# Splitting the first input load over two queues and moving a bias transpose in a fused attention and MLP kernel

One core of a Trainium2 chip. The metric is the device time of one execution in microseconds (us), median of several runs.

## The reference, cut to what matters

```python
x  = A_x                                # [1, 2048, 640] bf16
xn = layernorm(x)                       # per row of 640
return x + attention(xn, wqkv, wo) + mlp(xn, w1, b1, w2, b2)

def mlp(x, w1, b1, w2, b2):             # w1 [640, 1536], w2 [1536, 640]
    h = gelu_tanh(x @ w1 + b1)
    return h @ w2 + b2
```

The linear attention (32 heads) comes after the first MLP half in the kernel and is not touched by the change.

## The kernel before: the parts that matter

Tokens come in 16 tiles of 128 rows. The kernel starts with the MLP's first half on tiles 0 and 1, since that needs only x, W1 and the bias b1. The loads are issued from two queues, SyncE's and ScalarE's:

```python
KA = 2
dma_x(0, 1)                                                     # SyncE: x0, 128 rows
dma_w("scalar", b1tmp[:], B_b1..., r_b1tmp)                     # ScalarE: bias, 12 rows of 128
dma_w("scalar", W1[:, 0:KA, 0:FW], w1v[:, 0:KA, 0:FW], r_W1A)   # ScalarE: first W1 rows, 256 KB
dma_x(1, 1)                                                     # SyncE: x1
dma_w("sync", W1[:, KA:DT, 0:FW], w1v[:, KA:DT, 0:FW], r_W1[0]) # SyncE: rest of W1 block 0
dma_w1(1); dma_x(2, 1); dma_w1(2); dma_x(3, 1); ...             # SyncE: W1 block 1, x2, W1 block 2, x3
```

TensorE meanwhile multiplies zeros (`filler`), which does nothing but keep it active, and transposes the bias. VectorE takes the LayerNorm statistics of x0 and of x1, and then normalizes x0:

```python
filler(6)            # six zero matmuls of 512 columns
b1_step()            # bias transpose on TensorE, copy on ScalarE
filler(3)
ln_stats(0)          # VectorE, GpSimd: statistics of x0
ln_half(1, 0)        # VectorE: statistics of x1
ln_half(1, 1)
norm_part(0, 0, CA, r_xnA)      # VectorE: normalize x0, in two parts
norm_part(0, CA, D, r_xnB)
ln_aggr(1)
dA, sA, bA = transp_part(0, 0, 2, r_xnA)     # TensorE: transposes of x0
filler(1)
dB, sB, bB = transp_part(0, 2, DT, r_xnB)
# ... [cut] copies, normalize x1, transposes of x1, products of tile 0, of tile 1
units(0, 2, JQ, 2 * JQ + 1)     # from here on 256 tokens at once
```

## Time and profile before

| | before |
|---|---|
| time, median of 3 (range) | 206.53 us (206.44 to 206.76) |
| span of the profiled execution | 205.2 us |
| x0 landed / x1 landed | 3.15 / 3.83 us |
| x0 transposes / first products | 5.54 / 6.40 us |
| TensorE at full clock from | 4.96 us |

All times within an execution are counted from the start of its span. TensorE has work without a gap from 6.4 us to the end, so the end moves with anything that delays it there. "Landed" is the last of the semaphore increments of a load in the trace, one for each DMA engine that took part. The clock is the trace's record of the granted TensorE clock. The profile lines stand in the prediction.

### The profile page before, as it was taken

To read this page: it belongs to the slowest core of one execution; us is meant where nothing else is said; L and a number is where in the kernel's file an instruction comes from. 1 tells how busy PE (TensorE), PEld (TensorE's weight loads), DVE (VectorE), ACT (ScalarE), POOL (GpSimd) and SP (SyncE) were. 2 spreads that over 40 slices of the span, in tenths; PEclk is the share of its full clock that TensorE was granted. 3 is DMA by queue.
4 is the path that set the end of the run, shared out by engine and by line. 5 is a ranking of instruction groups with operands and counts; after the bars stand their busy time and mean duration, and the time that the engine had idled before them with its cause. 6 is when DMAs were issued, how large, how long until landed. Compare 5 with 4: busy or idle time off the path is not lost.

```text
span 205.2 us, 3767 instructions
## 1 busy us (share of the span) xinstructions
PE 201.8 (98%) x1517; PEld 138.6 (68%) x1517; DVE 113.2 (55%) x231; ACT 72.5 (35%) x136; POOL 15.0 (7%) x46
## 2 busy tenths in 40 slices
PE   7999999999999999999999999999999999999996
PEld 2789987444457777777756565677777777777775
DVE  4678677200006888999388888464773422523332
ACT  3588887666676554211143675000000000000000
POOL 3143334300000000000000000000000000000000
PEclk9999999999999999999999999999999999999999
DMA  5993954499940000000300034781112111010012
GB/s 181 350 352 79 70 96 91 78 355 268 285 164 0 0 0 3 0 0 3 64 0 2 3 71 89 244 279 43 67 64 71 54 43 50 32 35 32 32 35 66
DMA packets 26664, 19.23 MB, mean 94 GB/s; under 512 B 13766, under 2 KB 26646, under 8 KB 26646
## 3 DMA queue, kind: packets, MB, share of 16 engines
q1 hardware_dynamic: 26350, 18.72, 33.5%
q10 hardware_dynamic: 296, 0.27, 0.4%
q8 instruction: 12, 0.20, 0.4%
q14 instruction: 6, 0.05, 0.1%
HBM read 12.72 MB, written 2.62 MB: 75 GB/s over the span
## 4 chain that ended last, share of the span: by engine, by line
PE 96%; DVE 1%; DMA 1%; issue 0%; DVEq 0%
PE ps L644 34%; PE ps L358 24%; PE ps L495 11%; PE ps L531 11%; PE ps L543 11%; PE ps L680 2%; PE ps L390 1%; DMA xPK<-in_A_x_dram 1%; DVE stats L314 1%; PE ps L557 1%; PE ps L575 1%; PE ps L591 1%; PE ps L379 0%; PE ps L342 0%; DVE xn_tm L372 0%
## 5 line engine op out<-in xcount | busy, mean ns | idle before, releaser
L644 PE MATMUL ps<-W,HG 128*128 128x320 bf16 x360 | 51.0, 300 | 0.0
L358 PE MATMUL ps<-xnT,W 128*128 128x256 bf16 (+2 forms) x385 | 50.6, 294 | 0.0
L644 PEld LDWEIGHTS ps<-W,HG 128*128 128x128 bf16 x360 | 35.1, 98 | 14.2 <-issue 0.4
L358 PEld LDWEIGHTS ps<-xnT,W 128*128 128x128 bf16 x385 | 33.8, 98 | 16.0 <-DMA W<-in_B_w_dram 0.2
L362 ACT ACTIVATE HG<-ps,b1c 128x256 bf16<-128x256 f32 (+2 forms) x77 | 38.0, 515 | 12.8 <-PE ps L358 10.4
L663 DVE TENSOR_TENSOR out_sb<-ps,xnT 128x640 bf16<-128x640 f32 x15 | 12.4, 825 | 35.0 <-PE ps L644 33.6
L482 ACT ACTIVATE ek<-ps 128x512 bf16<-128x512 f32 (+1 forms) x36 | 23.2, 644 | 19.6 <-PE ps L543 10.4
L483 DVE TENSOR_SCALAR ek<-ek 128x512 bf16<-128x512 bf16 (+1 forms) x36 | 11.0, 307 | 26.3 <-ACT ek L482 24.8
L543 PE MATMUL ps<-xnT,Wqkv 128*128 128x512 bf16 x100 | 22.8, 380 | 0.0
L644 PE MATMUL ps<-Msb,PQ 128*128 128x320 bf16 x150 | 22.3, 300 | 0.0
L495 PE MATMUL ps<-Wqkv,xnT 128*128 128x320 bf16 x160 | 21.9, 300 | 0.0
L531 PE MATMUL ps<-xPK,xn_tm 128*128 128x320 bf16 x160 | 21.9, 300 | 0.0
L495 PEld LDWEIGHTS ps<-Wqkv,xnT 128*128 128x128 bf16 x160 | 15.7, 98 | 6.2
L531 PEld LDWEIGHTS ps<-xPK,xn_tm 128*128 128x128 bf16 x160 | 15.7, 98 | 6.1
L644 PEld LDWEIGHTS ps<-Msb,PQ 128*128 128x128 bf16 x150 | 14.7, 98 | 5.7
L543 PEld LDWEIGHTS ps<-xnT,Wqkv 128*128 128x128 bf16 x100 | 11.3, 118 | 8.5
L314 DVE BATCH_NORM_STATS2 stats<-xPK 128x6 f32<-128x320 bf16 x32 | 14.7, 469 | 3.1 <-DMA xPK<-in_A_x_dram 3.1
L485 DVE SCALAR_TENSOR_TENSOR PQ<-ps,ek 128x512 bf16<-128x512 f32 x20 | 13.8, 692 | 2.1
L485 DVE SCALAR_TENSOR_TENSOR xPK<-ps,ek 128x640 bf16<-128x640 f32 x16 | 13.2, 825 | 1.7
L518 DVE TENSOR_TENSOR Msb<-Msb,xPK 128x640 f32<-128x640 f32 x14 | 11.6, 825 | 0.5
L324 POOL TENSOR_TENSOR rstd<-aggr,mhalf 128x1 f32<-128x1 f32 x16 | 9.1, 567 | 15.8 <-DVE aggr L322 15.8
L535 ACT ACTIVATE W<-ps 128x640 bf16<-128x640 f32 x5 | 3.5, 703 | 18.2 <-PE ps L531 18.2
(61 smaller groups left out, 90.5 us busy)
## 6 DMA issues: line engine op xcount, KB each, us to landing
xnT<-in_A_x_dram SPq DMA_DIRECT2D x4, 640.0 KB, 6.8
Wqkv<-in_A_wqkv_dram SPq DMA_DIRECT2D x3, 800.0 KB, 6.6
out_dram<-out_sb SPq DMA_DIRECT2D x15, 160.0 KB, 1.8
W<-in_B_w_dram SPq DMA_DIRECT2D x1, 1920.0 KB, 15.8
W<-in_B_w_dram SPq DMA_DIRECT2D x2, 640.0 KB, 7.4
xPK<-in_A_x_dram SPq DMA_DIRECT2D x2, 640.0 KB, 9.0
Wo<-in_A_wo_dram SPq DMA_DIRECT2D x1, 750.0 KB, 12.4
xPK<-in_A_x_dram SPq DMA_DIRECT2D x4, 160.0 KB, 4.6
```

What stands on the lines that cost most here:

```text
L314: Pl.ins(v, lambda e: e.bn_stats(stats[:, s, 6 * h:6 * h + 6], x_in[:, t, h * HW:(h + 1) * HW]), reads=[r_x[t]], writes=[r_stats[s][h]])
L358: Pl.ins("tensor", [(lambda e, k=k: e.matmul(bank(b, 0, w), W1[:, k, jb * P:(jb + 1) * P], xnT[:, k, tok], start=(k == 0), stop=(k == DT - ...
L362: Pl.ins("scalar", lambda e: e.activation(HG[:, jb, tok], bank(b, 0, w), ACT.Gelu_apprx_tanh, bias=b1c[:, jb:jb + 1]), reads=[B_[b], r_b1c ...
L482: Pl.ins("scalar", lambda e: e.activation(e2, src, ACT.Exp), reads=br, writes=[r_ek[s]])
L483: Pl.ins(v, lambda e: e.tensor_scalar(et, et, 1.0, 1e-6, ALU.min, ALU.add), reads=[r_ek[s]], writes=[r_ek[s]])
L485: Pl.ins(v, lambda e: e.scalar_tensor_tensor(out=d2, in0=src, scalar=0.0, in1=e2, op0=ALU.max, op1=ALU.add), reads=br + [r_ek[s]], writes= ...
L495: fns.append(lambda e, k=k, h=h, b=b, t=t: e.matmul(bank(b + h, 0, HW), xnT[:, k, t * P:(t + 1) * P], Wqkv[:, k, D + h * HW:D + (h + 1) * ...
L518: Pl.ins(v, lambda e, t=t: e.tensor_tensor(out=zsum, in0=zsum, in1=PK[:, t, :], op=ALU.add), reads=[r_PK[t], r_zsum], writes=[r_zsum])
L531: Pl.ins("tensor", [(lambda e, t=t, h=h, b=b, f=f: e.matmul(bank(b + h, 0, HW), xn_tm[:, t, f * P:(f + 1) * P], PK[:, t, h * HW:(h + 1) * ...
L543: Pl.ins("tensor", [(lambda e, k=k, j=j, b=b: e.matmul(bank(b), Wqkv[:, k, j:D:DT], xnT[:, k, cc], start=(k == 0), stop=(k == DT - 1))) fo ...
L644: return lambda e: e.matmul(bank(b + h, 0, HW), l, r[:, h * HW:(h + 1) * HW], start=(i == 0), stop=(i == JT + DT - 1))
L663: Pl.ins(v, lambda e: e.tensor_tensor(out=halves(out_sb[:, s, :]), in0=pair(b), in1=halves(x_res[:, t, :]), op=ALU.add), reads=B_[b:b + 2] ...
```

## The change

The intent: x0 is the first load and everything waits for it, so let two queues bring one half each; bring the first W1 rows directly behind; let the small bias come later, as it is needed last. Its transpose moves behind the zero matmuls, of which eight stand ahead of LayerNorm instead of nine.

```diff
-        dma_x(0, 1)
+        HP = P // 2
+        r_x0b = R_("x0b")
+        dma_w("sync", x_in[0:HP, 0, :], xv[0:HP, :], r_x[0])
+        dma_w("scalar", x_in[HP:P, 0, :], xv[HP:P, :], r_x0b)
+        dma_w("scalar", W1[:, 0:KA, 0:FW], w1v[:, 0:KA, 0:FW], r_W1A)
         dma_w("scalar", b1tmp[:], B_b1.rearrange("(a p) -> a p", p=P), r_b1tmp)
-        dma_w("scalar", W1[:, 0:KA, 0:FW], w1v[:, 0:KA, 0:FW], r_W1A)
         dma_x(1, 1)
 # ... [cut: the statistics of x0 wait for r_x0b as well]
-        filler(6)
+        filler(8)
         b1_step()
-        filler(3)
         ln_stats(0)
```

More of the change, by code (lines that the diff above doesn't have):

```diff
@@ L314, in ln_half @@
             Pl.ins(v, lambda e: e.bn_stats(stats[:, s, 6 * h:6 * h + 6], x_in[:, t, h * HW:(h + 1) * HW]),
-                   reads=[r_x[t]], writes=[r_stats[s][h]])
+                   reads=[r_x[t]] + ([r_x0b] if t == 0 else []), writes=[r_stats[s][h]])
             if h == 0:
```

## The prediction

> **What bounds the kernel now.** I read the page's busy shares first, then the chain of work that ended last, then the start of the trace engine by engine, because the change touches nothing after the first 6 us. Shares and the 40 slices:
>
> ```profile
> span 205.2 us, 3767 instructions
> PE 201.8 (98%) x1517; PEld 138.6 (68%) x1517; DVE 113.2 (55%) x231; ACT 72.5 (35%) x136; POOL 15.0 (7%) x46
> ...
> PE   7999999999999999999999999999999999999996
> ```
>
> TensorE holds the end. It is short of full only in the first slice (5.1 us) and the last, so a change to the loads can win only part of the first 6 us, about 3% of the span. The first pieces of the chain, in order of time, give that part its order (columns: start, length, what, all us):
>
> ```profile
> 0.80 2.35 DMA xPK<-in_A_x_dram
> ...
> 3.17 0.90 DVE stats L314 x2
> ...
> 5.14 0.36 DVE xn_tm L372
> ...
> 5.54 0.29 PE ps L379 x2
> ...
> 6.40 0.94 PE ps L390 x14
> ```
>
> The first x tile is issued at 0.80 and lands at 3.15. LayerNorm of it follows on VectorE and GpSimd (3.17 to 5.50), then the transposes from 5.54, then the first real matmuls at 6.40. So x0's landing looks like the bound, and 3.25 us of fixed work lie between it and the first product (6.40 - 3.15). The same stretch on TensorE, in the timeline:
>
> ```profile
> 1.25 2.74 PE L301 MATMUL ps<-warm 128*128 128x512 bf16 x6 [1.25 <-DVE warm L270]
> 3.92 0.19 PE L306 MATMUL ps<-ident,b1tmp 12*128 12x12 bf16 x1
> 4.04 1.25 PE L301 MATMUL ps<-warm 128*128 128x512 bf16 x3
> 5.54 0.29 PE L379 MATMUL ps<-ident,xn_tm 128*128 128x128 bf16 x2 [0.25 <-DVE xn_tm L372]
> ```
>
> Nine zero matmuls and the bias transpose end at 5.29; TensorE is idle for 0.25 us before the x0 transposes, so none of those is on the path. Most important for me is what comes later: two waits for loads that the change does not shorten, one in the weight loads of TensorE, one on VectorE.
>
> ```profile
> 11.34 0.44 PEld L358 LDWEIGHTS ps<-xnT,W 128*128 128x128 bf16 x5 [0.17 <-DMA W<-in_B_w_dram]
> ```
>
> ```profile
> 9.46 0.89 DVE L314 BATCH_NORM_STATS2 stats<-xPK 128x6 f32<-128x320 bf16 x2 [1.09 <-DMA xPK<-in_A_x_dram]
> 11.41 0.45 DVE L335 TENSOR_SCALAR xn_tm<-xPK,aggr,rstd 128x640 bf16<-128x640 bf16 x1 [0.76 <-POOL rstd L324]
> ```
>
> The third block of W1 (issued at 3.29, landed 8.0 us later, at 11.29) is needed by hidden block 8 at just that time: the weight load waits 0.17 us for it, which costs the matmuls some 0.05 us (their starts are 0.159 us apart there, 0.109 before). x2 lands at 9.43, and its LayerNorm ends at 11.86 (11.41 + 0.45), as TensorE comes to its transposes (11.91). TensorE therefore meets the load stream at 11.3 to 11.9 with no slack. After that it has no gap.
>
> **What the Trainium skill says.** "DMA: Bandwidth & Descriptors", section "Issuing engines are not separate DMA queues": loads from ScalarE's and SyncE's queues run on the same 16 DMA engines, and a second issuer saves only issue time. The trace fits: the order in which data moved (x0, x1, first W1 rows, rest of the block) is the order of issue over both queues (0.80, 1.25, 1.45, 1.72). The same page, "Queues, rings and completion order" and "Why a DMA increments its semaphore by 16 and not by 1": each engine works through one queue's descriptors in order, 128 or 64 rows are spread over 16 engines, 12 rows over the lowest 12. Fitting it, the bias tile has 12 landings after its issue in the trace (2.13 to 2.64), x0 has 16 (2.69 to 3.15). "TensorE: Matmul & The Clock Gate", Part 1: the array starts at half clock and is released after some 3.4 us of activity, in a window that does not start with the kernel. Here zero matmuls of 512 columns start 0.43 us apart at first, and the clock record goes to full at 4.96, 3.7 us after the first one.
>
> **The change, part by part.**
> 1. *x0 in two halves on two queues.* Of x0's 2.35 us, about 1.0 lie before its first bytes (they move at about 1.8), 1.0 are spent moving 160 KB, and the rest is landing. At the 300 GB/s of the filled queues, 160 KB would take 0.5 us, so the ramp is worth at most 0.5 us. Both halves still use all 16 engines, each with 4 rows per queue in place of 8 in one, and 16 more queue entries have to be made. The bias load no longer goes first. I expect 0.15 us (estimate; 0 to 0.35), so landing at 3.0.
> 2. *The chain behind it* moves along unchanged: transposes at 5.39 instead of 5.54, first products at 6.25 instead of 6.40. Its limit is the first W1 rows: 15 of their 16 landings came by 4.91, the last, from one slow engine, at 6.04 (1.45 + 4.6). So at most 0.3 us can be won there. They remain second on ScalarE's queue and are issued at about the same time.
> 3. *Zero matmuls.* 9 become 8 ahead of LayerNorm: 1.25 + 8 x 0.43 = 4.69 for their end. The removed 0.43 us lay in idle time: no gain. The clock may be released later because TensorE is idle from about 4.9 to 5.4; I give that little weight.
> 4. *The bias*, now third on ScalarE's queue, issued near 1.86, some 1.06 us later than before, and one more issue of 0.4 to 0.6 us before the 1.28 us table load. ScalarE is idle from 4.33 to 5.87, so that is hidden. But the bias now stands behind the W1 rows on each of its 12 engines, and TensorE must do its transpose (0.19 us) before those of x0. If the slow engine is not among the 12, it lands near 4.3 to 5.0 and costs nothing. If it is, it lands near 6.1.
> 5. *Bytes.* The load stream up to x2 and the third W1 block has the same bytes and, on SyncE, the same number of issues. It lands earlier only by what the ramp saves: 0 to 0.15 us.
>
> Sum: the front wins 0.15 us, but TensorE then meets the third W1 block and x2 earlier and waits for them. What reaches the end is the advance of the stream, about 0.05 us, plus the 0.05 us already lost there if all goes well. From 206.53 that is 206.4; the bias risk moves the middle back to 206.5.
>
> **Rivals.**
> A. *The gain arrives whole*: x0 0.3 us earlier, stream with it, 206.2. For it: the chain begins with this load, and the first half microsecond of transfers is thin. Against it: the wait at 11.34 and x2's landing.
> B. *The bias becomes the wait*: TensorE takes its instructions in order, so a bias at 6.1 puts the x0 transposes at 6.25 or so instead of 5.54, and a delay, unlike a gain, passes the meeting at 11.3 almost whole: +0.65, 207.15. For it: a slow engine shows in nearly every load up to 17 us, and 12 of 16 engines carry the bias. Against it: the engine may be one of the four others, and its W1 rows may come sooner in the new order. Chance 0.3; smaller delays (bias at 5.5, +0.1) are included in the range.
> C. *The clock*: with 0.43 us less work early, release comes one window later; the first 60 or so short matmuls (up to 9 us) would run at half rate, about +1 us, 207.5. The zero matmuls still fill 1.25 to 4.69, so chance 0.07.
>
> **Range and chances.** About 0.6 for the hidden gain (206.3 to 206.6), 0.1 for A, 0.3 for some delay. Middle 206.5, 8 in 10 between 206.1 and 207.1. 2% is 4.1 us: even A is a tenth of that, and B and C stay at or under 1 us, so "same" is all but sure.
>
> **What would show it.** Right, if: x0's statistics start at 2.85 to 3.15 instead of 3.17; the bias transpose ends before the first x0 transpose could start; the wait for the third W1 block near 11.3 grows from 0.17 us by about what the first products gained; the x2 statistics start within 0.15 us of 9.46; VectorE, not the bias, ends TensorE's idle time before L379's successor. Wrong, if the bias load ends that idle time (B), if short matmuls after 6.3 us start 0.107 us apart (C), or if the third W1 block and x2 land over 0.2 us earlier and the end moves with them (A).

## The result, and the profile after

| | before | after |
|---|---|---|
| time, median of 6 runs (range) | 206.72 us (206.44 to 206.95) | 208.81 us (207.62 to 208.94) |
| ratio, 95% interval | | 1.0086, 1.0057 to 1.0115 |
| span of the profiled execution | 205.2 us | 206.3 us |
| x0 landed / x1 landed | 3.15 / 3.83 us | 3.49 / 5.08 us |
| first W1 rows / bias landed | 6.04 / 2.64 us | 4.80 / 5.29 us |
| x0 transposes / first products | 5.54 / 6.40 us | 6.29 / 7.14 us |

A ratio here and below is the mean time of one kernel's runs over that of the other's runs of the same rounds, so it is not quite the ratio of the medians.

The change costs some 2 us at the median, and its times fall into two groups: 207.62 and 207.68 in one, 208.74 to 208.94 in the other. The profile of after, taken in an execution of 207.68, shows only the first group. VectorE's timeline (start, length, engine, line, operation; in brackets how long the engine had been idle and what ended it), first x1's statistics before, then three lines of that execution of after:

```profile
4.29 0.83 DVE L314 BATCH_NORM_STATS2 stats<-xPK 128x6 f32<-128x320 bf16 x2
```

```profile
3.52 0.89 DVE L317 BATCH_NORM_STATS2 stats<-xPK 128x6 f32<-128x320 bf16 x2 [2.32 <-DMA xPK<-in_A_x_dram]
5.10 0.89 DVE L317 BATCH_NORM_STATS2 stats<-xPK 128x6 f32<-128x320 bf16 x2 [0.39 <-DMA xPK<-in_A_x_dram]
5.91 0.74 DVE L375 TENSOR_SCALAR xn_tm<-xPK,aggr,rstd 128x256 bf16<-128x256 bf16 x2
```

The first line of after is x0's statistics, 0.35 us later than before (3.17). The second is x1's: VectorE waits for that load, and 5.10 compares with 4.29 before. The third, x0's normalization, starts as soon as VectorE has finished with x1. TensorE in the same execution, matmuls and then weight loads (PEld):

```profile
1.25 3.53 PE L304 MATMUL ps<-warm 128*128 128x512 bf16 x8 [1.25 <-DVE warm L273]
5.34 0.18 PE L309 MATMUL ps<-ident,b1tmp 12*128 12x12 bf16 x1 [0.56 <-DMA b1tmp<-in_B_b_dram]
6.29 0.28 PE L382 MATMUL ps<-ident,xn_tm 128*128 128x128 bf16 x2 [0.78 <-DVE xn_tm L375]
7.14 0.94 PE L393 MATMUL ps<-xnT,W 128*128 128x128 bf16 x14
```

```profile
10.09 2.08 PEld L361 LDWEIGHTS ps<-xnT,W 128*128 128x128 bf16 x20 [0.24 <-DMA W<-in_B_w_dram]
12.42 0.44 PEld L361 LDWEIGHTS ps<-xnT,W 128*128 128x128 bf16 x5 [0.25 <-DMA W<-in_B_w_dram]
```

The idle time ahead of the x0 transposes, 0.25 us before, is now 0.56 + 0.78 us, with the bias transpose in the middle. The bias ends the first wait; it does not hold up the x0 transposes, which wait for VectorE. They come 0.75 us late, and the first products 0.74 us. The 256-token products start at 10.09 instead of 9.11: those 0.74 and another 0.24 for the second W1 block. That is 0.98 of the span's +1.05. The queues show why x1 is late (x0 is taken up at e8). SyncE's and ScalarE's issues, before and then after (ACTq, SPq: time to issue; a line may hold two issues, x2):

```profile
0.80 0.87 SPq L234 DMA_DIRECT2D xPK<-in_A_x_dram  x2
0.80 0.62 ACTq L238 DMA_DIRECT2D b1tmp<-in_B_b_dram  x1
1.45 0.41 ACTq L238 DMA_DIRECT2D W<-in_B_w_dram  x1
```

```profile
0.80 0.59 SPq L238 DMA_DIRECT2D xPK<-in_A_x_dram  x1
1.45 0.80 SPq L234 DMA_DIRECT2D xPK<-in_A_x_dram  x1
0.81 0.55 ACTq L238 DMA_DIRECT2D xPK<-in_A_x_dram  x1
1.39 0.60 ACTq L238 DMA_DIRECT2D W<-in_B_w_dram  x1
2.02 0.68 ACTq L238 DMA_DIRECT2D b1tmp<-in_B_b_dram  x1
```

Before, x0 and x1 took 0.39 and 0.42 us to issue (0.87 with the pause) and x1's issue was over at 1.67. After, half an x0 takes 0.59, x1 behind it 0.80, and x1's issue is over at 2.25, after the W1 rows' (1.99). An issue on the other queue at the same time isn't enough to make it long: before, x1 (0.42) was issued beside the W1 rows as well. The data follow: W1 rows landed at 4.80, x1 at 5.08.

What the second group of times is remained to be found. The candidates were the loads (in some executions still later), the bias, and the clock.

### The profile page after: what moved, and what is told of

It is laid out like the page before. It is cut to its first block, busy times and chain, and to the rows that moved or that the text cites. A ratio compares the mean times of both kernels' runs of the same rounds, so it can differ in the third digit from the quotient of the medians.

```text
span 206.3 us, 3761 instructions
## 1 busy us (share of the span) xinstructions
PE 201.3 (98%) x1509; PEld 138.7 (67%) x1516; DVE 113.3 (55%) x231; ACT 72.7 (35%) x136; POOL 15.0 (7%) x46
## 4 chain that ended last, share of the span: by engine, by line
PE 94%; DMA 4%; SPq 1%; issue 0%; DVE 0%
PE ps L646 34%; PE ps L361 24%; PE ps L533 11%; PE ps L497 11%; PE ps L545 10%; DMA W<-in_B_w_dram 4%; PE ps L682 2%; PE ps L559 1%; PE ps L577 1%; PE ps L593 1%; SPq L238 0%; SPq L234 0%; PE ps L345 0%; DVE out_sb L685 0%
## 5 line engine op out<-in xcount | busy, mean ns | idle before, releaser
L545 PE MATMUL ps<-xnT,Wqkv 128*128 128x512 bf16 x96 | 22.2, 379 | 0.2
L545 PEld LDWEIGHTS ps<-xnT,Wqkv 128*128 128x128 bf16 x100 | 11.3, 118 | 8.5
```

The lines of the kernel that those rows point to most:

```text
L545: Pl.ins("tensor", [(lambda e, k=k, j=j, b=b: e.matmul(bank(b), Wqkv[:, k, j:D:DT], xnT[:, k, cc], start=(k == 0), stop=(k == DT - 1))) fo ...
```

## The experiments

The theories: **load** (two queues issuing at once make issues longer and the load stream late), **bias** (TensorE held up by the bias transpose), **clock** (less work ahead of the first products, so the full clock is granted a window later in some executions). Times of before in the same rounds: 206.54 (e1 to e4), 206.66 (e5 to e8), 206.67 (e9, e10). e1 to e4 ran on one chip, e5 to e10 on another, each beside before on the same chip.

### e1: the changed kernel again

No edit.

> The changed kernel once more, for the spread of its two groups of times (207.65 in two runs, 208.7 to 208.9 in four) and, with luck, a profile of the slower group. Load theory (two queues issuing at once make each issue longer, so the stream of loads comes 1.1 us later): explains the 207.65 group only. Clock theory (fewer zero matmuls, so the full clock is granted one window later in some executions): a profile of the 208.8 group has short matmuls 0.107 us apart after 6.5 us, or a stretch of some 3 us at half clock.

Measured: 208.63, 207.93, 208.84, 209.06 us. With the six above, 7 of 10 executions are at 208.6 or more and 3 at 207.6 to 207.9. The profile was one of the slower group, 208.63. TensorE's timeline of it:

```profile
6.52 0.40 PE L382 MATMUL ps<-ident,xn_tm 128*128 128x128 bf16 x2 [0.96 <-DVE xn_tm L375]
7.48 1.68 PE L393 MATMUL ps<-xnT,W 128*128 128x128 bf16 x14
9.93 1.46 PE L393 MATMUL ps<-xnT,W 128*128 128x128 bf16 x20
11.23 2.89 PE L361 MATMUL ps<-xnT,W 128*128 128x256 bf16 x25
```

The 14 products that took 0.94 us take 1.68 here. The trace's clock record goes to full only at 9.71, against 4.96 in the profile of before. When TensorE comes to the 256-token products at 11.23 nothing makes it wait, for the second W1 block had landed at 9.24. x0 and x1 were 0.2 us later than in the fast profile (3.68 and 5.31), and the x0 transposes with them (6.29 there, 6.52 here); the larger part of the difference is in the lengths of the matmuls. So the slower group is not, in the main, one of later loads. Note that the page's mean granted clock says 1.0 for this execution: that mean doesn't see the clock before its first record. Here one has to look at the lengths of like matmuls.

### e2: the halves alone

```diff
+ halves of x0 on SyncE and ScalarE, as in the change
+ ScalarE then: bias, first W1 rows          (the order of before)
+ filler(6); b1_step(); filler(3)            (the order of before)
```

> x0 in two halves on two queues, but the bias ahead of the first W1 rows and the bias transpose amid nine zero matmuls, as before. Load theory: 207.7 (+1.1) or a bit more, with SyncE's second and third issues 0.6 us later and x2 landing near 10.5. Bias theory (the late bias holds up TensorE): as before, 206.7. Clock theory: no run of the slower group, whatever the loads do.

Measured: 206.78 us median (206.72 to 207.20), ratio 1.001 (0.9992 to 1.0027): not told apart from before. No slow group; full clock from 4.19. The load theory as I had put it falls: SyncE's issues are 0.6 us later here too (x1's over at 2.25), but x2 landed at 9.19, no later than before (9.43). The halves did not help either: x0 landed at 3.40 instead of 3.15, x1 at 4.60, and the x0 transposes start at 5.81 instead of 5.54.

### e3: the order of loads and zero matmuls, without halves

```diff
  dma_x(0, 1)
+ dma_w("scalar", W1[:, 0:KA, 0:FW], ..., r_W1A)
  dma_w("scalar", b1tmp[:], ..., r_b1tmp)
- dma_w("scalar", W1[:, 0:KA, 0:FW], ..., r_W1A)
- filler(6); b1_step(); filler(3)
+ filler(8); b1_step()
```

> x0 whole on SyncE's queue, first W1 rows and then the bias on ScalarE's, eight zero matmuls and then the bias transpose. Load theory: SyncE's issues as before, so 206.7 in the executions whose clock is released early. Bias theory: TensorE waits for the bias until 5.3 or later, +0 to +0.7. Clock theory: some executions 1.2 us slower than the others.

Measured: 206.76 and 206.82, and 207.95, 207.98, 207.99, 208.45 us: two groups some 1.2 us apart, as the clock theory says. Ratio 1.0048 (1.0020 to 1.0076). The bias landed at 4.52 and its transpose ran at 4.78, right behind the zero matmuls, so TensorE never waited for the bias in the profile, and that was one of a slow execution (208.45, full clock at 10.60). The bias theory falls for the slower group. The W1 rows ahead make x0 (3.38) and x1 (4.72) later here as well, and the x0 transposes wait 0.96 us.

### e4: the order of zero matmuls alone

```diff
- filler(6); b1_step(); filler(3)
+ filler(8); b1_step()
```

> All loads as before; eight zero matmuls and then the bias transpose. Load and bias theory: 206.7, no change. Clock theory: two groups, 206.7 and 207.9.

Measured: 206.34, 206.35, 206.76, 206.78, 206.82 and one of 208.05 us; ratio 1.0009 (0.9983 to 1.0035). So eight zero matmuls instead of nine are almost harmless while the loads are those of before: the idle time ahead of the x0 transposes is 0.55 us. It takes both, fewer zero matmuls and later loads, to make it long. (Before, too, had one execution of 207.64 in 11 in these rounds.)

### e5: the changed kernel with more zero matmuls

```diff
- filler(8)
+ filler(11)
  b1_step()
```

> The changed kernel with eleven zero matmuls ahead of the bias transpose instead of eight: they fill TensorE's idle time from 4.85 to the bias (5.3) and most of that up to the x0 transposes (6.3 to 6.5); loads as in the changed kernel. Clock theory (the clock is granted late where too much of an activity window is idle): the slower group vanishes, all executions near 207.6, what the later loads alone cost. If the loads alone cause both groups: unchanged, most executions at 208.7 to 209.

Measured: 207.33, 207.45, 207.45, 207.61 and, in the profiled execution, 208.05 us; ratio 1.0042 (1.0029 to 1.0056). Three useless matmuls make the changed kernel some 1.3 us faster at the median (207.45 against 208.81; e1, on another chip, has 208.74; e9 and e7 are a pair on one chip). In the 208.05 the clock came at 6.30, and the cause was another: x1's last increment came at 5.57, the bias's at 5.98 and that of the rest of W1 block 0 at 8.35, all from late engines.

### e6: the kernel before with fewer zero matmuls

```diff
  filler(6)
  b1_step()
- filler(3)
```

> The kernel before, loads and all, with the three zero matmuls behind the bias transpose taken out: TensorE is idle from 4.05 to 5.54, as long a gap as the changed kernel's. Nothing waits for those zero matmuls, so a reading of waits alone says 206.6. Clock theory: in most executions the clock is granted 3.4 us later, 207.7 to 208.2, the rest 206.6.

Measured: 207.50 to 208.04 us, median 207.84, ratio 1.0057 (1.0045 to 1.0070). All five executions are slower, the loads are as before (x0 landed at 3.11, x1 at 3.71), and no instruction waits for the matmuls removed. TensorE's timeline:

```profile
5.51 0.39 PE L379 MATMUL ps<-ident,xn_tm 128*128 128x128 bf16 x2 [1.39 <-DVE xn_tm L372]
6.47 1.68 PE L390 MATMUL ps<-xnT,W 128*128 128x128 bf16 x14
```

The transposes start when they did before, but the 14 products take 1.68 us; the full clock came at 9.80. This is the clock's cost by itself: 1.2 us.

### e7: the changed kernel, x0 normalized ahead of x1's statistics

```diff
  ln_stats(0)
- ln_half(1, 0); ln_half(1, 1)
  norm_part(0, 0, CA, r_xnA); norm_part(0, CA, D, r_xnB)
+ ln_half(1, 0); ln_half(1, 1)
```

> The changed kernel with VectorE normalizing x0 before it takes the statistics of x1. If x1's late landing (5.1, behind the first W1 rows) is what holds up x0's normalization, the x0 transposes start near 5.8 instead of 6.3 to 6.5, the idle gap shrinks to 0.5 + 0.3 us, and more than half of the executions are in the fast group, near 207.1. If not, nothing changes: 6.3 and 208.7.

Measured: 208.39 to 209.18 us, median 208.88. The x0 transposes did come forward, to 5.87, so x1's landing is what held up x0's normalization. The time did not follow: a miss. TensorE's timeline:

```profile
5.53 0.18 PE L309 MATMUL ps<-ident,b1tmp 12*128 12x12 bf16 x1 [0.76 <-DMA b1tmp<-in_B_b_dram]
5.87 0.28 PE L382 MATMUL ps<-ident,xn_tm 128*128 128x128 bf16 x2 [0.16 <-DVE xn_tm L375]
6.72 0.61 PE L393 MATMUL ps<-xnT,W 128*128 128x128 bf16 x8
7.70 0.58 PE L393 MATMUL ps<-xnT,W 128*128 128x128 bf16 x6 [0.38 <-DVE xnT L420]
9.65 2.11 PE L393 MATMUL ps<-xnT,W 128*128 128x128 bf16 x20
```

Here the clock was granted at 4.56, in the middle of the zero matmuls, taken back at 7.98 and granted again at 11.39: 8 products take 0.61 us, and the last 20 take 2.11, where they took 1.41 in the profile of after. The steps are 3.41 us apart. So there are two ways to a slow execution: a late grant, or an early one that is withdrawn. In the slower executions of after both seem to occur: two of the four have a mean granted clock of 0.992, as this one has, the other two 1.0, as e1's profile has.

### e8: both halves on SyncE's queue

```diff
  halves of x0, as in e2
- dma_w("scalar", x_in[HP:P, 0, :], ...)
+ dma_w("sync", x_in[HP:P, 0, :], ...)
  everything else as in e2
```

> x0 in two halves, both on SyncE's queue, bias and W1 rows on ScalarE's in the order of before, zero matmuls as before: as e2 but with one queue for the halves. If it is two queues issuing side by side that makes issues long (0.6 us each instead of 0.4) and x0 late, issues are 0.4 us here and x0 lands near 3.2 to 3.4. If the halving itself (more queue entries) costs it, x0 lands as in e2 (3.4) or later. End 206.6 to 206.9 either way.

Measured: 208.07, 208.91, 209.02, 209.11, 209.16 us, ratio 1.011 (1.0091 to 1.0128): far from the 206.6 to 206.9 expected. SyncE's issues:

```profile
0.80 1.24 SPq L238 DMA_DIRECT2D xPK<-in_A_x_dram  x2
2.09 0.58 SPq L234 DMA_DIRECT2D xPK<-in_A_x_dram  x1
```

The first line is the two halves, the second x1. The halves take 0.60 and 0.57 us to issue although they are on one queue. So a load of 64 rows took longer to issue than the whole x0 did before (0.39), whichever queue had it, and the first idea of my expectation, that it is the second queue, is refuted. x1, a whole 128 rows, takes long behind a half too: 0.58 here, with nothing issued beside it, and 0.80 in after and in e2. Why is open, and one rival was not tried: the halves come from another helper (`dma_w`) than the whole tile (`dma_x`), and no run issues a whole x0 by it.

The long issue alone does not make a load late either: the first half lands at 3.16, as x0 did before, and in these traces x0 lands later only where a load of 64 or 128 rows, and not the bias, is issued beside it (3.40 and 3.49 in halves, 3.38 and 3.49 whole in e3 and e10).

The second half is issued at 1.46, as the W1 rows are (1.45), and those land first (4.56); the half lands at 4.78. VectorE's and TensorE's timelines show what that costs:

```profile
4.88 0.89 DVE L317 BATCH_NORM_STATS2 stats<-xPK 128x6 f32<-128x320 bf16 x2 [3.68 <-DMA xPK<-in_A_x_dram]
```

```profile
7.25 0.29 PE L382 MATMUL ps<-ident,xn_tm 128*128 128x128 bf16 x2 [1.75 <-DVE xn_tm L375]
```

The second idea, that halving itself costs, came out stronger than thought. The profile is of the fastest execution (208.07); what adds another 0.8 to 1.1 us in the other four was not profiled.

### e9: the changed kernel with both mended

```diff
- filler(8)
+ filler(10)
  b1_step()
  (and the order of e7)
```

> The changed kernel with both suspected costs taken away: ten zero matmuls ahead of the bias transpose (idle time filled) and x0 normalized before x1's statistics (x1's late landing no longer in its way). Loads as in the changed kernel. If clock and x1 are the two causes, x0 transposes near 5.9, no late or withdrawn clock, and 206.8 to 207.1 in all executions: what is left is x0's later landing (0.35) and the load stream. If the loads themselves carry the +0.8 of e5, it stays at 207.4.

Measured: 207.76 to 208.28 us, median 207.81, ratio 1.0065 (1.0052 to 1.0077). The clock came at 6.25 and stayed, and the x0 transposes ran at 5.80. Against e7, which has the same order and loads and ran on the same chip, two more zero matmuls gain 1.1 us. Yet it is no faster than e5. VectorE's and TensorE's timelines:

```profile
5.40 0.76 DVE L375 TENSOR_SCALAR xn_tm<-xPK,aggr,rstd 128x256 bf16<-128x256 bf16 x2 [0.76 <-POOL rstd L327]
6.08 0.88 DVE L317 BATCH_NORM_STATS2 stats<-xPK 128x6 f32<-128x320 bf16 x2
8.04 0.76 DVE L375 TENSOR_SCALAR xn_tm<-xPK,aggr,rstd 128x256 bf16<-128x256 bf16 x2 [0.54 <-POOL rstd L327]
```

```profile
7.64 0.49 PE L393 MATMUL ps<-xnT,W 128*128 128x128 bf16 x6 [0.27 <-DVE xnT L420]
8.44 0.28 PE L382 MATMUL ps<-ident,xn_tm 128*128 128x128 bf16 x2 [0.31 <-DVE xn_tm L375]
10.36 2.89 PE L361 MATMUL ps<-xnT,W 128*128 128x256 bf16 x25
```

Normalizing x0 first put x1 back: its statistics run from 6.08, its normalization from 8.04 (7.53 in after, 6.79 before). What the x0 products gained is lost at x1 a little later, as TensorE needs both tiles before the 256-token products (10.36 here, 10.09 in the fast profile of after). The cause is no longer x1's landing: x1 was there at 5.31, but VectorE first waited 0.76 us for GpSimd, normalized x0, and came to x1 at 6.08. My expectation of 206.8 to 207.1 was wrong in taking x0 for the only one that counts.

### e10: e3 with more zero matmuls

```diff
- filler(8)
+ filler(10)
  b1_step()                    (loads as in e3)
```

> As e3 (x0 whole, first W1 rows and then the bias on ScalarE's queue), with ten zero matmuls instead of eight. Clock theory: all executions in e3's fast group, 206.7 to 206.9; the order of loads by itself costs at most 0.2. Otherwise 207.9 as in e3.

Measured: 206.63 to 206.88 us, median 206.74, ratio 1.0008 (0.9994 to 1.0021). The slower group of e3 is gone. The order of loads alone costs at most 0.2%.

### The clock, over all traces

From the matmuls and weight loads in a trace I summed TensorE's idle time in the 3.41 us that ended at each change of the clock, in the window of 3.41 us ahead of a late grant, and in the one after the grant ("slow" is the slower group of times).

| trace | full clock from | idle in the window that ended there | idle in the window ahead of it | idle in the window after it |
|---|---|---|---|---|
| before | 4.96 | 0% | | 9% |
| e2 | 4.19 | 14% | | 28% |
| e5 | 6.30 | 2% | | 20% |
| e8 | 6.00 | 15% | | 38% |
| e9 | 6.25 | 0% | | 18% |
| e10 | 5.11 | 0% | | 15% |
| e1 (slow) | 9.71 | 6% | 37% | 0% |
| e3 (slow) | 10.60 | 0% | 28% | 0% |
| e6 (slow) | 9.80 | 0% | 41% | 0% |
| e7 (slow) | 4.56, withdrawn at 7.98 | 3% | | 39% |

The windows lie differently from run to run, so the same kernel may meet a good or a bad one. The grant came with windows of up to 15% idle time and did not come with 28% or more. That TensorE's idle time early on decides over the 1.2 us is shown by e5 (against after), e6 (against before), e10 (against e3) and e9 (against e7): each pair differs in zero matmuls alone. What withdraws a clock once granted is open: e7 lost it after a window with 39% idle, e8 kept it after one with 38%. The traces of after and e4 have no clock record. In the fast profile of after the eighth zero matmul took 567 ns, against 634 for those wholly at the lower clock and 557 in e7, where the grant came 0.35 us after its start. From that I estimate the grant at 4.59; the window after it was 41% idle, and yet the products of 128 columns stay mostly 55 to 56 ns apart up to 9.8 (106 to 107 at the lower clock in e1). So the idle share of a window does not decide the withdrawal by itself.

## Why the prediction was wrong

Predicted 206.5 (206.1 to 207.1), measured 208.81. Two steps failed where it counts: step 2 in every execution (the loads, +0.8 us) and step 3 in most (the clock, +1.2 us). By its own steps:

1. **x0 in halves: "landing at 3.0". Wrong in sign.** It landed at 3.49 (3.40 in e2). The step names 16 more queue entries but gives their issue no time. A half took 0.55 to 0.60 us to issue, the whole x0 0.39; e8 shows that this alone does not delay the first half (3.16). Alone (e2) the halves cost the start of the x0 transposes 0.27 us.
2. **"The chain behind it moves along unchanged." Wrong.** The step that failed in the fast executions. VectorE takes x1's statistics ahead of x0's normalization. Before, x1 was there in time (3.83); in the prediction its landing does not occur, though what it calls 3.25 us of fixed work contains x1's statistics. The chain that it quotes had the line, `4.38 0.76 DVE stats L314 x2`; it was left out there under one of the "...". After, its issue ends after that of the W1 rows and it lands at 5.08, so the first products start 0.74 us late. The first W1 rows, which the prediction took for the next limit, were early (4.80). In e7, with x0 normalized first, the x0 transposes come at 5.87 instead of 6.29, which shows it.
3. **"The clock may be released later ...; I give that little weight." Wrong in weight.** This is rival C, given a chance of 0.07 and +1 us. By their times it happened in 7 of 10 executions (one of them profiled, e1), and its size was 1.2 us (e6). The prediction had the idle time after the zero matmuls as 4.9 to 5.4; it became 4.78 to 6.29, or 4.85 to 6.52 in e1, but for the bias transpose, because of step 2.
4. **The bias (rival B, chance 0.3). Half right.** It did land late, at 5.29, behind the W1 rows, and its wait shows in the profile; but VectorE's x0 came later still. It has no cost of its own that a run showed. As idle time it adds to step 3.
5. **The load stream "earlier by 0 to 0.15". Not seen.** x2 landed at 10.51 and 9.70 in two profiles of after, 9.43 before. In the fast execution this added 0.24 us of waiting for the second W1 block (landed 10.04), in the slow one nothing. Why that block's last engine is so late in several runs with the order of the change (10.04, 10.15, 9.76) and not in e2 (8.72) is open.

Right was that the change stays within 2%, and that a delay, unlike a gain, passes on to the end: TensorE has no slack after 6.4 us. e10 starts its first products 0.48 us later than before and its profiled span ends 0.4 us later.

The sum, as far as runs show it: loads +0.8 (e5 over before, 207.45 against 206.66), clock +1.2 to 1.4 in most executions, together the 2.1 between the medians. No version that I ran beats the kernel before. Nor is one in sight from these runs, though that is argued and not tried: even with x0 sooner, TensorE meets the third W1 block at 11.3 and x2 at 11.9, as the prediction's views show.

## What to carry to other kernels

Matmuls that nothing waits for may still be on the path: before taking out or moving filler work, count TensorE's idle time in every stretch as long as the clock's window, and not only the waits. Splitting a small first load can make it later: here each half took longer to issue than the whole, and an issue on another queue changes which load goes first; check the landing of the second and third load that the engines' program order needs, not of the first alone. When a kernel's times fall into two groups, get a profile of each group before explaining either.

## What the Trainium skill lacked or had wrong

- "TensorE: Matmul & The Clock Gate", "Why this matters for your kernels", advises against idle gaps of more than about 3 us between bursts of matmuls. Here much shorter gaps were enough: in e7 the clock was withdrawn after a window with gaps of at most 0.76 us, 39% idle in sum; in e6 a single gap of 1.39 us put off the grant to 9.80. The window itself (3413 ns, Part 1) agrees: 3.41 us between changes in e7.
- The same page, Part 1, reports a kernel that lost the full clock through frequent short idle times, but does not say how full a window has to be. The runs show grants at up to 15% idle and none at 28% to 41%. A clock once granted was kept at 38% (e8) and withdrawn at 39% (e7).
- The same part puts the warm-up penalty below 1% of a typical kernel and advises against fitting a count of slow matmuls. Below 1% is right (one window more cost 1.2 us of 206.7, 0.6%), but it is more than half of this change's whole effect.
- No page that I read gives issue times by the number of rows: the halves took 0.55 to 0.60 us to issue, the whole x0 0.39, and x1 behind a half 0.58 to 0.80 instead of 0.42. "DMA: Bandwidth & Descriptors", "Issuing engines are not separate DMA queues", says that issuing from a second engine saves sequencer time, and that holds between the halves on one queue (e8, x1's issue over at 2.67) and on two (e2, 2.25); against the whole x0 (before, 1.67) it does not make up for the halving.
